# Joining the softmax of two head groups and moving the value products back in a two-layer attention and Fourier kernel

## The chip, the cores and the metric

The kernel runs on one core of a Trainium2 chip. The metric is the device time of one execution in microseconds.

## The reference

The input x has 2048 rows of 640 columns. Four layers follow each other, each adding to x a function of its layer norm: attention, Fourier mixing, attention, Fourier mixing, with the same weights in both of a kind.

```python
x = x + _A_ref(_layernorm(x), A_wqkv, A_wo)
x = x + _B_ref(_layernorm(x), ...)      # and both once more
# _A_ref: 32 heads of 20 columns; row s looks at rows s, s-2, ..., s-14
logits = einsum("bhsd,bhswd->bhsw", q, kg) * scale      # 8 keys per row
attn = softmax(where(mask, logits, -1e9));  o = einsum("bhsw,bhswd->bhsd", attn, vg);  o @ wo
# _B_ref: real part of a DFT over columns and rows, as matrix products
y = einsum("ts,bse->bte", seq_re, a) - einsum("ts,bse->bte", seq_im, b)
```

## The kernel before

Rows are held in 4 chunks (c) of 4 x 128 rows (j). Matrix products are made in three passes of high and low parts, so each operand is split once by ScalarE (high) and VectorE or GpSimd (low). TensorE makes the query/key/value products (`qkv_mm`, L365: 64 groups of 15 matmuls per attention layer), transposes of 128 x 128 (L330) with the subtraction that yields their low part (`pc_sub`, L338), the output projection (`wo_mm`, L518), and the first product of the Fourier layer that follows (`z_mm`, L976), which is begun before the attention layer has ended.

The local attention itself is elementwise work. Keys and values go out to memory and come back as windows, so that each partition holds 4 rows with the 11 rows that their 8 keys span. A head group u (32 per layer: 8 groups of 4 heads for each chunk) is worked in two halves, jp = 0 and 1. For each half:

- `qk_mul` (L434, VectorE): the query times 8 keys, 1280 elements per partition. GpSimd then adds the two halves of each head's 20 columns (L437), except in the half-steps listed in `WHOLE`.
- `qk_red` (L444, VectorE): sums what is left, 640 elements (1280 for a whole one), to 64 logits.
- `soft` for the group: mask (L459, only chunks 0 and 2), maximum over 8 keys (L461), subtraction (L463), the exponential on ScalarE (L452), sum (L465), reciprocal (L467), weights p (L469).
- `av_mul` (L474, VectorE): p times 8 values, 1280 elements. `av_tree` then sums over the keys, on GpSimd in three steps (L493 to L495), and in one step on VectorE (L490) for the very last half.

The order is written out by hand. `at(step, phase, fn, ...)` enters work into a plan; the plan is then issued by half-step, and in each by the list `PHASES`, so that every engine's queue has a fixed order. The query product of group u and half jp stands in half-step s = 2u + jp, its reduction in s + 1, the softmax in 2u + 2 (mask, maximum, subtraction, exponential) and 2u + 3 (sum, reciprocal, weights), the value product in s + 3. `OUTP` has the half-steps in which finished rows of chunks 0 and 1 are transposed (the projection follows two and three later, `wo_add` L162 one after each), `LNS` those of the layer norm of the next layer, `ZTHIRDS` how many thirds of a z product stand in each half-step (from 49 in the first attention layer, from 50 in the second). The query/key/value products are spread by a loop of their own and end in half-steps 47 and 49.

Query (`qp`), weights (`pp`), maximum, sum and mask lie in one PSUM tile `pq`; the logits `lg` in SBUF, in two buffers; products in four SBUF buffers `pr`, windows in five buffers `win`.

Of the kernel before, what the change touches and what calls it, by code (L numbers as in the profile page):

```python
# [22 lines left out]
DH = 20  # L23
W = 8
# [24 lines left out]
ZTHIRDS = (  # L49
    {49: 3, 50: 3, 51: 2, 52: 1, 53: 2, 54: 1, 56: 3, 57: 6, 58: 3, 59: 4, 60: 2, 61: 1, 62: 3, 63: 4, 64: 1},  # L50
    {50: 3, 51: 5, 52: 1, 53: 1, 54: 1, 55: 1, 56: 5, 57: 4, 58: 3, 59: 3, 60: 1, 61: 1, 62: 4, 63: 2, 64: 4},
)
TA = 65
NWARM = 18
# [23 lines left out]
def tile_layers(ctx: ExitStack, tc: tile.TileContext, x, wqkv, wo, cs, wre, wim, out):  # L78
# [166 lines left out]
    def layer_a(li, stats, handoff, prev):  # L245
# [11 lines left out]
        win = {}  # L257
        lgs = {}
        prq = {}
# [41 lines left out]
        def tp(step, kind, c, j, k0, k1, bank, col=0, tag=None):  # L301
            if step not in pieces:
                pieces[step] = []
                at(step, "peT0", pc_pe, step)
                at(step, "hi", pc_hi, step)
                at(step, "peL2" if step == 46 else "peL", pc_sub, step)
                at(step, "actL", pc_lo, step)
            pieces[step].append((kind, c, j, k0, k1, bank, col, tag))
# [132 lines left out]
        def qk_red(u, jp):  # L441
            if jp == 0:
                lgs[u] = T([P, NJ, W, HE], "lg", bufs=2)
            nc.vector.tensor_reduce(  # L444
                lgs[u][:, 2 * jp : 2 * jp + 2].rearrange("p j w h -> p (j w h)"),
                prq.pop((u, jp)),
                axis=AX.X,
                op=ALU.add,
            )

        def soft_exp(u):
            nc.scalar.activation(lgs[u], lgs[u], AF.Exp, scale=scale)  # L452

        def soft(u, part):
            lg = lgs[u]
            v = nc.vector
            if part == 0 and (u // NE) % 2 == 0:
                mw = bass.AP(tensor=mk.tensor, offset=mk.offset, ap=[mk.ap[0], [1, NJ], [1, W], [0, HE]])
                v.tensor_tensor(lg, lg, mw, op=ALU.add)  # L459
            if part == 1:  # L460
                v.tensor_reduce(mx, lg.rearrange("p j w h -> p j h w"), axis=AX.X, op=ALU.max)  # L461
            if part == 2:
                v.tensor_tensor(lg, lg, mx.unsqueeze(2).to_broadcast([P, NJ, W, HE]), op=ALU.subtract)  # L463
            if part == 3:
                v.tensor_reduce(sm, lg.rearrange("p j w h -> p j h w"), axis=AX.X, op=ALU.add)  # L465
            if part == 4:
                v.reciprocal(sm, sm)  # L467
            if part == 5:
                v.tensor_tensor(pp, lg, sm.unsqueeze(2).to_broadcast([P, NJ, W, HE]), op=ALU.mult)  # L469
                lgs[u] = pp  # L470

        def av_mul(u, jp):
            pr = prod()
            nc.vector.tensor_tensor(  # L474
                pr.rearrange("p j w (h d) -> p j w h d", d=DH),
                lgs[u][:, 2 * jp : 2 * jp + 2].unsqueeze(4).to_broadcast([P, 2, W, HE, DH]),
                wview(u, jp, 1, [[DH, HE], [1, DH]]),
                op=ALU.mult,
            )
            avq[(u, jp)] = pr  # L480

        def av_tree(u, i):
            c = u // NE
            e, jp = half(u, i)
            if e == 0:
                oo[(c, jp)] = T([P, 2, D], f"zo{(2 * c + jp) % 4}")
            pr = avq.pop((u, i))
            o = oo[(c, jp)][:, :, e * FE : (e + 1) * FE]
            if (u, i) == (NG - 1, 1):
                nc.vector.tensor_reduce(o, pr.rearrange("p j w f -> p j f w"), axis=AX.X, op=ALU.add)  # L490
# [4 lines left out]
            g.tensor_tensor(o, pr[:, :, 0], pr[:, :, 1], op=ALU.add)  # L495
# [195 lines left out]
        o = NJ * FE + NJ * W * HE  # L691
        mx = pq[:, o : o + NJ * HE].rearrange("p (j h) -> p j h", j=NJ)
        sm = pq[:, o + NJ * HE : o + 2 * NJ * HE].rearrange("p (j h) -> p j h", j=NJ)
        mk = pq[:, o + 2 * NJ * HE : o + 2 * NJ * HE + SLOTS]
        for i in range(3 if first else 0):
# [40 lines left out]
        for u in range(NG):  # L736
            if u in PAIRED:
                for i in range(2):
                    at(2 * u + i - 2, "dmaw", w_load, u, 0, i)
                    at(2 * u + i + 1, "dmaw", w_load, u, 1, i)  # L740
# [47 lines left out]
        for c, w, xtags in (  # L788
            (2, (52, 53, 54, 55), None),
            (3, (60, 61), ("xa", "xa")),  # L790
        ):
            for j in range(NJ):
                if c == 2:
                    late = j > 2 and not first
                    bank = ("xt", "t0", "t1", "t0" if late else "m0")[j]
                    tp(50 if late else 48, "o", c, j, 0, 3, bank, 0, ("ot", "s1", "r1_2", "r1_2")[j])
                    tp(52, "o", c, j, 3, 5, f"aux{j // 2}", 256 * (j % 2))
                else:
                    tp(58 if j < 2 else TA, "o", c, j, 0, 3, f"aux{j % 2}", 0, ("ot", "s1", "zo0", "zo1")[j])
                    tp(60 if j < 2 else 67, "o", c, j, 3, 5, "aux0" if j < 2 else "pq", 256 * (j % 2))  # L800
                if j < len(w):
                    if xtags:
                        at(58, "dmar", r_load, c, j, xtags[j])
                    at(w[j], "pe3w", wo_mm, c, j, ("aux1", "aux0") if c == 3 else ("aux0", "aux1"))
# [7 lines left out]
        for ph in ("peT0", "hi", "peL", "actL"):  # L812
            plan.pop((67, ph))
        at(66, "pe3w", wo_mm, c, 2, ("aux0", "aux1"), 0, 2, 0, 3)
        for i in range(2):
            at(65, "dmas", *((handoff.cw_load, 0) if first else (handoff.c_get,)), 14 + i)
        at(65, "dmar", r_load, c, 2, "xr")
        at(66, "dmar", r_load, c, 3, "xa")
# [11 lines left out]
        for z in range(len(thirds) // 3):  # L830
            t = thirds[3 * z]
            if first and z in PRE:
                at((46, 47, 49)[z] if z < 3 else max(thirds[3 * z - 7] + 1, t - 3), "dmac", handoff.c_get, z)
            elif first:
# [3 lines left out]
            else:  # L838
                at(min(t - 1, 48 + z) if z < 3 else t - 1, "dmac", handoff.c_get, z)
            for p in range(3):  # L840
                at(thirds[3 * z + p], "pe2" if thirds[3 * z + p] == 52 else "pe3", handoff.z_mm, z, p)
        if first:
            at(62, "dmac", handoff.c_load, 13)
            at(63, "hi", handoff.c_hi, 13)
            at(63, "misc", handoff.c_lo, 13)
        else:
            at(63, "dmac", handoff.c_get, 13)

        PHASES = (
            "peT0 dma evac hi pe peL pe2 peL2 fin red0 dma2 qk sA sB av0 sD red1 sE sC exp evacA actL chi evacO actl sF av1 qc actz"  # L850
            " dmaw dmas misc dmac dmar pe3w pe3"
        ).split()
        with tc.manual_schedule(engines=ENGINES):
            if first:
                prologue_first()
            nc.vector.tensor_copy(mk, mask)
# [4 lines left out]
            pc_pe(67)  # L861
            pc_hi(67)
            pc_lo(67, True)
            wo_mm(c, 2, None, 0, 2, 3)
# [517 lines left out]
```

## Time and profile before

| | before |
|---|---|
| median of 3 runs | 1772.23 us (1769.08 to 1773.06) |
| profiled execution | 1771.33 us |
| its span | 1769.3 us |
| granted TensorE clock, mean | 0.995 |
| TensorE busy | 1736.0 us (98%) |
| VectorE busy | 1388.5 us (78%) |
| ScalarE busy | 810.8 us (46%) |
| GpSimd busy | 624.6 us (35%) |

Busy times are unions over the span of one execution. In the rows below PE is TensorE, PEld its weight loads, DVE VectorE, ACT ScalarE, POOL GpSimd and SP SyncE, which issues most DMAs. A group's row has line, engine, operation, tiles (out<-in), shapes and count, then total busy us and mean ns of one, then the engine's idle time just before them and what ended it. A row of the waits has who waited for whom, us in total, times, and the longest. A timeline row has start and duration in us. A row of the windows view has, for a stretch of the span, each engine's busy time and number of instructions, TensorE's granted clock, the DMA share and GB/s.

### The profile page before, as it was taken

The numbers are of one execution on the slowest core, as the hardware profiler recorded it, in microseconds if no ns is written. First come the engines' busy times: TensorE is split into PE (matmuls) and PEld (weight loads), VectorE is DVE, ScalarE is ACT, GpSimd is POOL, SyncE is SP. The second block draws the span as 40 slices with busy tenths as digits, with TensorE's granted clock in tenths as the row PEclk, the third lists the DMA queues.
The fourth block names the chain that finished last, engine by engine and source line by source line (L and its number), as shares of the span: only waits on it lengthen the run. The fifth ranks groups of instructions, "written<-read, shape, count | busy, mean of one in ns | idle before, by whom it ended". The sixth has DMA issues, their size and how long they took to land.

```text
span 1769.3 us, 26448 instructions
## 1 busy us (share of the span) xinstructions
PE 1736.0 (98%) x8798; PEld 1505.9 (85%) x8798; DVE 1388.5 (78%) x2127; ACT 810.8 (46%) x1686; POOL 624.6 (35%) x587
## 2 busy tenths in 40 slices
PE   9999998989999999999999999999999999999999
PEld 6889897878888888888898889988788888888888
DVE  5999999977767767767548999999777676686673
ACT  4654544554445445445534344444434443443441
POOL 3899988850000000000028998899200000000000
PEclk9999999999999999999999999999999999999999
DMA  7996769858777787786657866698688767867761
GB/s 269 309 325 212 220 202 311 274 170 277 274 254 232 243 269 232 246 270 222 206 185 223 264 213 219 202 334 275 203 283 290 247 211 243 260 218 239 255 203 53
DMA packets 270760, 426.19 MB, mean 241 GB/s; under 512 B 22528, under 2 KB 149504, under 8 KB 270368
## 3 DMA queue, kind: packets, MB, share of 16 engines
q1 hardware_dynamic: 267424, 422.54, 72.3%
q10 hardware_dynamic: 3200, 1.97, 0.4%
q8 instruction: 70, 1.15, 0.3%
q14 instruction: 66, 0.54, 0.1%
HBM read 339.28 MB, written 85.14 MB: 240 GB/s over the span
## 4 chain that ended last, share of the span: by engine, by line
PE 59%; DVE 20%; DMA 9%; POOL 5%; issue 4%; ACT 3%; SPq 0%; DVEq 0%; ACTq 0%; POOLq 0%
PE aux L1058 13%; PE t L1147 11%; PE m L1147 11%; PE m L365 9%; PE pq L1147 5%; PE xt L1147 5%; DVE pr L434 4%; DVE pr L474 3%; DMA xc<-stg 3%; PE aux L518 3%; DVE lg L444 2%; POOL pr L493 2%; DMA win<-kvb 1%; POOL pr L437 1%; DVE stg L1111 1%
## 5 line engine op out<-in xcount | busy, mean ns | idle before, releaser
L365 PE MATMUL m<-r,s 128*128 128x480 f32 x1920 | 436.2, 381 | 2.7 <-ACT r L129 2.2
L365 PEld LDWEIGHTS m<-r,s 128*128 128x128 f32 x1920 | 355.4, 188 | 56.3 <-ACT r L129 2.7
L1058 PE MATMUL aux<-r2a,zo 128*128 128x320 f32 x768 | 226.5, 310 | 0.0
L1140 ACT CAST r<-win 128x512 fp32r<-128x512 f32 x246 | 150.5, 620 | 158.4 <-DVE win L1176 75.4
L493 POOL TENSOR_TENSOR pr<-pr 128x640 f32<-128x640 f32 x126 | 208.2, 1652 | 37.3 <-DVE pr L474 36.7
L1058 PE MATMUL aux<-pr,zo 128*128 128x320 f32 x704 | 208.3, 308 | 0.0
L177 POOL TENSOR_TENSOR stats<-stats,mhalf 128x1 f32<-128x1 f32 (+1 forms) x40 | 29.0, 726 | 493.8 <-ACT stats L173 484.7
L1141 DVE TENSOR_TENSOR r<-win,r 128x512 fp32r<-128x512 f32 x246 | 166.3, 688 | 45.0 <-ACT r L1140 43.8
L434 DVE TENSOR_TENSOR pr<-pq,win 128x1280 f32<-128x1280 f32 x128 | 189.7, 1483 | 9.7 <-ACT stg L372 4.8
L474 DVE TENSOR_TENSOR pr<-pq,win 128x1280 f32<-128x1280 f32 x128 | 190.7, 1491 | 4.9
L437 POOL TENSOR_TENSOR pr<-pr 128x640 f32<-128x640 f32 x118 | 168.8, 1431 | 16.2 <-DVE pr L434 15.7
L1147 PE MATMUL m<-r,r 128*128 128x512 f32 x594 | 152.6, 392 | 0.0
L1058 PEld LDWEIGHTS aux<-r2a,zo 128*128 128x128 f32 x768 | 144.1, 188 | 2.0
L1147 PE MATMUL t<-r,r 128*128 128x512 f32 x498 | 135.1, 393 | 1.7 <-PE t L1147 1.7
L1058 PEld LDWEIGHTS aux<-pr,zo 128*128 128x128 f32 x704 | 132.2, 188 | 2.1
L1147 PEld LDWEIGHTS m<-r,r 128*128 128x128 f32 x594 | 111.4, 188 | 24.7
L976 PE MATMUL m<-s,r 128*128 128x512 f32 x384 | 119.8, 400 | 4.0 <-DVE zo L1038 1.5
L976 PE MATMUL t<-s,r 128*128 128x512 f32 x384 | 118.2, 395 | 0.3 <-DVE ot L1033 0.3
L494 POOL TENSOR_TENSOR pr<-pr 128x320 f32<-128x320 f32 x126 | 111.8, 887 | 9.9
L444 DVE TENSOR_REDUCE lg<-pr 128x64 f32<-128x640 f32 (+1 forms) x128 | 110.5, 863 | 4.7 <-POOL pr L437 4.6
L1147 PEld LDWEIGHTS t<-r,r 128*128 128x128 f32 x498 | 93.4, 188 | 23.7 <-PE t L1147 2.5
L372 ACT COPY stg<-m 128x480 f32<-128x480 f32 x128 | 70.9, 554 | 69.5 <-PE m L365 50.2
(290 smaller groups left out, 3233.1 us busy)
## 6 DMA issues: line engine op xcount, KB each, us to landing
win<-cs_in SPq DMA_DIRECT2D x351, 256.0 KB, 4.3
r<-xc SPq DMA_DIRECT2D x240, 256.0 KB, 4.3
win<-kvb SPq DMA_DIRECT2D x96, 440.0 KB, 5.6
xa<-cs_in SPq DMA_DIRECT2D x121, 256.0 KB, 3.9
win<-kvb SPq DMA_DIRECT2D x64, 360.0 KB, 4.5
xc<-stg SPq DMA_DIRECT2D x40, 512.0 KB, 4.2
kvb<-stg SPq DMA_DIRECT2D x60, 320.0 KB, 5.3
s<-c0b SPq DMA_DIRECT2D x26, 512.0 KB, 6.1
```

The source lines that it names most:

```text
L365: nc.tensor.matmul(mt[g][:, : 3 * F], st[:, a, k], wq[q][:, b, k], start=n == 0, stop=n == 14)
L434: nc.vector.tensor_tensor(pr, q, wview(u, jp, 0, [[1, FE]]), op=ALU.mult)
L437: nc.gpsimd.tensor_tensor(pv[:, :, 0:10], pv[:, :, 0:10], pv[:, :, 10:20], op=ALU.add)
L444: nc.vector.tensor_reduce(lgs[u][:, 2 * jp : 2 * jp + 2].rearrange("p j w h -> p (j w h)"), prq.pop((u, jp)), axis=AX.X, op=ALU.add,)
L474: nc.vector.tensor_tensor(pr.rearrange("p j w (h d) -> p j w h d", d=DH), lgs[u][:, 2 * jp : 2 * jp + 2].unsqueeze(4).to_broadcast([P, 2, ...
L493: g.tensor_tensor(pr[:, :, 0:4], pr[:, :, 0:4], pr[:, :, 4:8], op=ALU.add)
L494: g.tensor_tensor(pr[:, :, 0:2], pr[:, :, 0:2], pr[:, :, 2:4], op=ALU.add)
L976: self.last = nc.tensor.matmul(self.z[t][k], self.xn[c][:, a, j, k * P : (k + 1) * P], self.ct[s][:, b], start=s == 0 and i == 0, stop=s = ...
L1058: self.last = nc.tensor.matmul(self.ym[e][:, :320], zt[(k, a, ri)][:, j2 * P : (j2 + 1) * P], w[:, e * 320 : (e + 1) * 320], start=(k, a, ...
L1140: nc.scalar.copy(hi, raw)
L1141: nc.vector.tensor_tensor(lo, raw, hi.bitcast(F32), op=ALU.subtract)
L1147: nc.tensor.matmul(bank, w(a, kb), hl[b], start=start and (a, b) == (0, 0), stop=stop and (a, b) == (1, 0),)
```

## The change

- The logits of two neighbouring groups (u even and u + 1) go into one buffer `lgr`, and mask, maximum, subtraction, exponential, sum and reciprocal are issued once for both, in half-steps 2u + 2 and 2u + 3 of the odd group. The weights p are still made group by group (`soft_p`).
- The value product of half-step s moves from s + 3 to s + 5, the load of its window with it. Output projections of chunks 0 to 3, layer norms, z products and their loads stand two half-steps later; a layer has two half-steps more. The query/key/value products stay.
- `WHOLE` becomes every fourth half-step (7, 11, ..., 63) in both layers: there VectorE reduces all 1280 elements, without GpSimd's half-add. Before there were 8 such half-steps in the first attention layer and 2 in the second.
- The sums over keys go to VectorE for two halves of a layer instead of one.
- In `PHASES` the sum, reciprocal and weights now stand ahead of the reduction of the same half-step.

```diff
-OUTP = (((20, 24, 28, 32), (36, 40, 44, 46)), ((20, 24, 28, 32), (36, 40, 44, 46)))
-LNS = ((40, 52), (42, 52))
+OUTP = (((22, 26, 30, 34), (38, 42, 46, 48)), ((22, 26, 30, 34), (38, 42, 46, 48)))
+LNS = ((42, 54), (44, 54))
-WHOLE = ((43, 45, 47, 49, 51, 55, 57, 59), (51, 57))
+WHOLE = ((7, 11, 15, 19, 23, 27, 31, 35, 39, 43, 47, 51, 55, 59, 63), (7, 11, 15, 19, 23, 27, 31, 35, 39, 43, 47, 51, 55, 59, 63))
 ZTHIRDS = (
-    {49: 3, 50: 3, 51: 2, 52: 1, ...
+    {51: 3, 52: 3, 53: 2, 54: 1, ...
...
         def qk_red(u, jp):
-            if jp == 0:
-                lgs[u] = T([P, NJ, W, HE], "lg", bufs=2)
+            n = 2 * W * HE
             nc.vector.tensor_reduce(
-                lgs[u][:, 2 * jp : 2 * jp + 2].rearrange("p j w h -> p (j w h)"),
+                lgr[:, u % 2, jp * n : (jp + 1) * n],
...
-        def soft_exp(u):
-            nc.scalar.activation(lgs[u], lgs[u], AF.Exp, scale=scale)
+        def soft_exp():
+            nc.scalar.activation(lgr, lgr, AF.Exp, scale=scale)
         def soft(u, part):
+            cols = lgr.rearrange("p b (j w h) -> p (b j) h w", j=NJ, w=W)
...
             if part == 1:
-                v.tensor_reduce(mx, lg.rearrange("p j w h -> p j h w"), axis=AX.X, op=ALU.max)
+                v.tensor_reduce(sm, cols, axis=AX.X, op=ALU.max)
...
             if part == 3:
-                v.tensor_reduce(sm, lg.rearrange("p j w h -> p j h w"), axis=AX.X, op=ALU.add)
+                v.tensor_reduce(sm, cols, axis=AX.X, op=ALU.add)
             if part == 4:
                 v.reciprocal(sm, sm)
-            if part == 5:
-                v.tensor_tensor(pp, lg, sm.unsqueeze(2).to_broadcast([P, NJ, W, HE]), op=ALU.mult)
-                lgs[u] = pp
+        def soft_p(u):
+            lg = lgr[:, u % 2].rearrange("p (j w h) -> p j w h", j=NJ, w=W)
+            r = sm[:, u % 2 * NJ : (u % 2 + 1) * NJ]
+            nc.vector.tensor_tensor(pp, lg, r.unsqueeze(2).to_broadcast([P, NJ, W, HE]), op=ALU.mult)
...
-            if (u, i) == (NG - 1, 1):
+            if i and u >= NG - 2:
                 nc.vector.tensor_reduce(o, pr.rearrange("p j w f -> p j f w"), axis=AX.X, op=ALU.add)
                 return
...
+        lgr = T([P, 2, NJ * W * HE], "lg")
...
                 at(2 * u - 2, "dmaw", w_load, u, 0)
-                at(2 * u + 1, "dmaw", w_load, u, 1)
+                at(2 * u + 3, "dmaw", w_load, u, 1)
...
-                at(s + 3, "av0" if jp else "av1", av_mul, u, jp)
-                at(s + 3, "av0" if jp else "av1", av_tree, u, jp)
-            for i, ph in enumerate(("sA", "sB", "sC")):
-                at(2 * u + 2, ph, soft, u, i)
-                at(2 * u + 3, ("sD", "sE", "sF")[i], soft, u, 3 + i)
-            at(2 * u + 2, "exp", soft_exp, u)
+                at(s + 5, "av0" if jp else "av1", av_mul, u, jp)
+                at(s + 5, "av0" if jp else "av1", av_tree, u, jp)
+            at(2 * u + 5, "sF", soft_p, u)
+            if u % 2:
+                for i, ph in enumerate(("sA", "sB", "sC")):
+                    at(2 * u + 2, ph, soft, u, i)
+                for i, ph in enumerate(("sD", "sE")):
+                    at(2 * u + 3, ph, soft, u, 3 + i)
+                at(2 * u + 2, "exp", soft_exp)
...
-        last = 66
+        last = 68
...
-            "peT0 dma evac hi pe peL pe2 peL2 fin red0 dma2 qk sA sB av0 sD red1 sE sC exp evacA actL chi evacO actl sF av1 qc actz"
+            "peT0 dma evac hi pe peL pe2 peL2 fin red0 dma2 qk sA sB av0 sD sE sF red1 sC exp evacA actL chi evacO actl av1 qc actz"
             " dmaw dmas misc dmac dmar pe3w pe3"
```

More of the change, by code (lines that the diff above doesn't have):

```diff
@@ L257, in layer_a @@
         win = {}
-        lgs = {}
         prq = {}
@@ L305, in tp @@
                 at(step, "hi", pc_hi, step)
-                at(step, "peL2" if step == 46 else "peL", pc_sub, step)
+                at(step, "peL2" if step == 48 else "peL", pc_sub, step)
                 at(step, "actL", pc_lo, step)
@@ L795, in layer_a @@
                     bank = ("xt", "t0", "t1", "t0" if late else "m0")[j]
-                    tp(50 if late else 48, "o", c, j, 0, 3, bank, 0, ("ot", "s1", "r1_2", "r1_2")[j])
-                    tp(52, "o", c, j, 3, 5, f"aux{j // 2}", 256 * (j % 2))
-                else:
-                    tp(58 if j < 2 else TA, "o", c, j, 0, 3, f"aux{j % 2}", 0, ("ot", "s1", "zo0", "zo1")[j])
-                    tp(60 if j < 2 else 67, "o", c, j, 3, 5, "aux0" if j < 2 else "pq", 256 * (j % 2))
+                    tp(52 if late else 50, "o", c, j, 0, 3, bank, 0, ("ot", "s1", "r1_2", "r1_2")[j])
+                    tp(54, "o", c, j, 3, 5, f"aux{j // 2}", 256 * (j % 2))
+                else:
+                    tp(60 if j < 2 else TA, "o", c, j, 0, 3, f"aux{j % 2}", 0, ("ot", "s1", "zo0", "zo1")[j])
+                    tp(62 if j < 2 else 69, "o", c, j, 3, 5, "aux0" if j < 2 else "pq", 256 * (j % 2))
                 if j < len(w):
                     if xtags:
-                        at(58, "dmar", r_load, c, j, xtags[j])
+                        at(60, "dmar", r_load, c, j, xtags[j])
                     at(w[j], "pe3w", wo_mm, c, j, ("aux1", "aux0") if c == 3 else ("aux0", "aux1"))
@@ L812, in layer_a @@
         for ph in ("peT0", "hi", "peL", "actL"):
-            plan.pop((67, ph))
-        at(66, "pe3w", wo_mm, c, 2, ("aux0", "aux1"), 0, 2, 0, 3)
+            plan.pop((69, ph))
+        at(68, "pe3w", wo_mm, c, 2, ("aux0", "aux1"), 0, 2, 0, 3)
         for i in range(2):
-            at(65, "dmas", *((handoff.cw_load, 0) if first else (handoff.c_get,)), 14 + i)
-        at(65, "dmar", r_load, c, 2, "xr")
-        at(66, "dmar", r_load, c, 3, "xa")
+            at(67, "dmas", *((handoff.cw_load, 0) if first else (handoff.c_get,)), 14 + i)
+        at(67, "dmar", r_load, c, 2, "xr")
+        at(68, "dmar", r_load, c, 3, "xa")
         if prev is not None:
@@ L855, in layer_a @@
                 prologue_first()
-            nc.vector.tensor_copy(mk, mask)
+            nc.vector.tensor_copy(
+                mk.rearrange("p (j w) -> p j w", j=NJ),
+                bass.AP(tensor=mask.tensor, offset=mask.offset, ap=[mask.ap[0], [1, NJ], [1, W]]),
+            )
             for s in range(LEAD0[0], last + 1):
@@ L860, in layer_a @@
                         fn(*args)
-            pc_pe(67)
-            pc_hi(67)
-            pc_lo(67, True)
+            pc_pe(69)
+            pc_hi(69)
+            pc_lo(69, True)
             wo_mm(c, 2, None, 0, 2, 3)
```

43 lines of the change are left out of this document (22 added, 21 removed).

## The prediction

> **What bounds the kernel now.** I read the page first, then the windows view cut at the borders of the stages, then VectorE's timeline over one step pair, the groups by form, and the waits by stage.
>
> ```profile
> span 1769.3 us, 26448 instructions
> PE 1736.0 (98%) x8798; PEld 1505.9 (85%) x8798; DVE 1388.5 (78%) x2127; ACT 810.8 (46%) x1686; POOL 624.6 (35%) x587
> ```
> ```profile
> core 0: us, PE busy (x) PEld busy (x) DVE busy (x) ACT busy (x) POOL busy (x), PEclk, DMA share, GB/s
> 35.30:279.40 244.10, 239.13 (x1233) 210.83 (x1232) 232.96 (x321) 131.81 (x328) 217.87 (x201) 1.00 0.80 257
> 279.40:359.10 79.70, 73.98 (x387) 64.70 (x388) 75.50 (x111) 35.78 (x91) 68.32 (x65) 0.96 0.82 279
> 918.90:960.10 41.20, 41.20 (x200) 35.76 (x199) 34.21 (x47) 14.94 (x33) 28.83 (x26) 1.00 0.71 226
> 960.10:1160.70 200.60, 200.03 (x1057) 178.49 (x1055) 191.47 (x272) 86.17 (x213) 182.99 (x168) 1.00 0.73 231
> 1160.70:1232.30 71.60, 68.24 (x361) 59.59 (x362) 66.97 (x101) 32.71 (x84) 66.05 (x62) 0.98 0.90 309
> ```
>
> Over the span TensorE looks like the only bound. The windows say more. I cut them where a query product starts. The first attention layer runs from half-step 0 (35.30) to 49 (279.40), where the first Fourier product (z) is planned, and on to 63 (359.10); the second from half-step 0 (918.90) over 9 (960.10) and 50 (1160.70, its first z) to 63 (1232.30). In the stretches ahead of z three engines are full together: in 960.10:1160.70 TensorE 99.7%, VectorE 95%, GpSimd 91%. Only from 918.90 to 960.10 is TensorE alone: VectorE works 34.21 of 41.20 us there. So a change of VectorE's load ahead of z counts, unless TensorE is behind it.
>
> VectorE's order, over half-steps 20 and 21 of the second layer:
>
> ```profile
> 1011.30 1.48 DVE L434 TENSOR_TENSOR pr<-pq,win 128x1280 f32<-128x1280 f32 x1
> 1012.82 0.39 DVE L461 TENSOR_REDUCE pq<-lg 128x16 f32<-128x128 f32 x1
> 1013.24 1.49 DVE L474 TENSOR_TENSOR pr<-pq,win 128x1280 f32<-128x1280 f32 x1
> 1014.65 0.28 DVE L463 TENSOR_TENSOR lg<-lg,pq 128x128 f32<-128x128 f32 x1
> 1014.85 1.48 DVE L434 TENSOR_TENSOR pr<-pq,win 128x1280 f32<-128x1280 f32 x1
> 1016.43 0.39 DVE L465 TENSOR_REDUCE pq<-lg 128x16 f32<-128x128 f32 x1
> 1016.73 0.81 DVE L444 TENSOR_REDUCE lg<-pr 128x64 f32<-128x640 f32 x1
> 1017.46 0.26 DVE L467 RECIPROCAL pq<-pq 128x16 f32<-128x16 f32 x1
> 1017.75 0.29 DVE L469 TENSOR_TENSOR pq<-lg,pq 128x128 f32<-128x128 f32 x1
> 1018.08 1.49 DVE L474 TENSOR_TENSOR pr<-pq,win 128x1280 f32<-128x1280 f32 x1
> 1019.51 0.82 DVE L444 TENSOR_REDUCE lg<-pr 128x64 f32<-128x640 f32 x1
> 1020.25 1.48 DVE L434 TENSOR_TENSOR pr<-pq,win 128x1280 f32<-128x1280 f32 x1
> ```
>
> Instructions overlap, so I cost them by the distance from start to start. The pair takes 1020.25 - 1011.30 = 8.95 us with no wait in it, four half-steps 17.90. Softmax's own distances: maximum 0.42, subtraction 0.20, sum 0.30, reciprocal 0.29, weights (L469) 0.33.
>
> **Softmax of two groups.** Wider forms are not in the trace; their slopes come from these groups:
>
> ```profile
> L444 DVE TENSOR_REDUCE lg<-pr 128x64 f32<-128x640 f32 x118 | 95.7, 811 | 4.7 <-POOL pr L437 4.6
> L465 DVE TENSOR_REDUCE pq<-lg 128x16 f32<-128x128 f32 x64 | 25.2, 394 | 8.1 <-ACT lg L452 2.0 <-ACT xa L194 0.5
> L461 DVE TENSOR_REDUCE pq<-lg 128x16 f32<-128x128 f32 x64 | 25.0, 391 | 2.1
> L444 DVE TENSOR_REDUCE lg<-pr 128x64 f32<-128x1280 f32 x10 | 14.8, 1476 | 0.0
> L490 DVE TENSOR_REDUCE zo<-pr 128x160 f32<-128x1280 f32 x2 | 4.7, 2360 | 0.1
> ```
>
> Where the reduced elements are neighbours (the two L444), an element costs (1476 - 811) / 640 = 1.04 ns. Where they lie apart, as in the maximum (stride 4) and in L490 (stride 80), it is (2360 - 391) / 1152 = 1.71 ns. The new maximum and sum reduce 256 elements at stride 4, so I take 128 x 1.71 = 0.22 us more each; the lower end, at the neighbours' slope, is 0.13. The subtraction grows by 128 x 1.04 = 0.13, the reciprocal, of 16 elements more, by an estimated 0.10 (between 0 and its own 0.26); the mask, in half of the groups, I set even. The exponential widens on ScalarE:
>
> ```profile
> L452 ACT ACTIVATE lg<-lg 128x128 f32<-128x128 f32 x64 | 20.1, 314 | 141.7 <-DVE lg L463 141.7
> ```
>
> It runs under the query product of 1.48 us that follows the subtraction. Only behind the last pair no query product follows; there it shows, at 0.31 us or up to twice that.
>
> [...]
>
> The order matters too. Reciprocal now follows the sum at once and needs its result, so the sum shows in full: 0.39 + 0.22 + 0.04 = 0.65 instead of twice 0.30. The next reduction writes where the weights' instruction has just read; the built program makes it wait, so that instruction still costs 0.33. Four half-steps then are: 1.52 + 0.64 + 1.41 + 0.33 = 3.90; 1.58 + 0.65 + 0.39 + 0.33 + 0.73 + 1.43 + 0.74 = 5.85; 1.41 + 1.41 = 2.82; 1.52 + 0.33 + 0.73 + 1.43 + 0.74 = 4.75. Sum 17.32: 0.58 saved.
>
> **Every fourth query product whole.** The reduction grows from 811 to 1476 ns: 0.67 per four half-steps. So VectorE's pace is 17.99 against 17.90, 0.09 slower: one edit pays for the other. GpSimd loses its half-add (L437), a quarter of them. What VectorE waited for it goes to nothing: 2.1 us in the first layer, 0.8 in the second.
>
> ```profile
> DVE lg L444 <- POOL pr L437: 2.1, 4, 0.9
> ```
> ```profile
> DVE pr L434 <- ACT pq L407: 1.6, 2, 1.5
> DVE r L910 <- ACT r L906: 1.0, 2, 0.5
> DVE lg L444 <- POOL pr L437: 0.8, 2, 0.6
> ```
>
> The first fence holds all of VectorE's waits between 60 and 299 us, the second the longest between 960 and 1160 us.
>
> **Two half-steps later.** The query/key/value products keep their steps and end at 47 (first layer) and 49. Out-projections, norms and z move by two together, with their loads, and keep their order on the SP queue. Only a group's value window is now issued behind the key window and the query of the group after next. It costs nothing while two half-steps (8.95 us) cover its landing, 5.6 us in the middle; without that cover VectorE's value product and all behind it would wait, as once for a key window:
>
> ```profile
> win<-kvb SPq DMA_DIRECT2D x96, 440.0 KB, 5.6
> ```
> ```profile
> DVE pr L434 <- DMA win<-kvb: 0.7, 1, 0.7
> ```
>
> But between the last key/value product and z TensorE now has two half-steps with little more than 15 matmuls of 2.36 us each, against 3.55 and 5.40 us of VectorE. And z can't come early, because the out-projection ahead of it waits for VectorE's addition:
>
> ```profile
> 270.20 2.36 PE L518 MATMUL aux<-r2a,ot 128*128 128x320 f32 x15
> ...
> 279.52 2.47 PE L518 MATMUL aux<-r2a,s 128*128 128x320 f32 x15 [0.45 <-DVE xr L162]
> 281.83 1.56 PE L976 MATMUL m<-s,r 128*128 128x512 f32 x6
> ```
>
> So z starts when VectorE has gone through two more half-steps: +8.95. From this, per layer:
> - First layer: the value products that half-steps 3 and 4 no longer hold free 2 x 1.41 = 2.8 (0 if TensorE were behind there; VectorE's 232.96 of 244.10 says it is mostly not). The old order had three whole sums by then (43, 45, 47), now inside the pace: -2.0. Pace 11.5 x 0.09 = +1.0; GpSimd's waits -2.1. Sum 8.95 - 2.8 - 2.0 + 1.0 - 2.1 = **+3.0**.
> - Second layer: its start is TensorE's (34.21 of 41.20), so the freed 2.8 only become idle time and count nothing. No whole sum stood ahead of z. Pace 10 x 0.09 = +0.9; GpSimd's waits -0.8; of the 2.6 on ScalarE I take half, -1.3. Sum 8.95 + 0.9 - 0.8 - 1.3 = **+7.7**.
>
> **From z on** the same matmuls follow, and TensorE sets the pace (73.98 of 79.70 and 68.24 of 71.60 busy), so VectorE's lighter load brings little: between 0 and the 9 us of gaps, I take -1.5, since most gaps wait for transposes that move along. **The tail** loses stalls on GpSimd:
>
> ```profile
> PE aux L330 <- POOL zo L495: 3.5, 2, 2.8
> PE pq L330 <- POOL zo L495: 1.7, 1, 1.7
> PE m L976 <- POOL s L963: 1.3, 1, 1.3
> ```
>
> Of these 2.8, 1.7 and 1.3 stand in the two tails, 5.8 together. GpSimd has no half-add left there, but VectorE now sums two value products whole (2360 ns each) and comes late in its place: between 0 and -5.8, I take -3.4.
>
> **Sum:** 3.0 + 7.7 - 1.5 - 3.4 = +5.8 us. The profiled execution took 1771.33 us (span 1769.3 and 2.0 around it), 0.9 below the median of 1772.23. So 1771.3 + 5.8 = 1777.1. A measurement of this kernel can tell about 0.2% from no change, 3.5 us.
>
> **Rivals.**
> - The strided reductions widen at the neighbours' slope: 2 x 0.09 less per pair, over 21.5 pairs 3.9 us, total +1.9, 1773. The 391 ns for 128 elements, far over what 1.04 ns each explain beside L444's remainder of 146 ns, speak against. [...] With half of the tail's gain lost it ends at 1775, still within 0.2%. Chance of such an end 0.22.
> - Faster: TensorE is the bound throughout (98%) and brings a backlog to the last key/value product, so that the two half-steps hide behind it. It decides from a backlog of 9 us on. Then z does not move, and 1.5 + 5.8 us of gaps go: 1764. For it: 200.03 of 200.60 us busy ahead of the second layer's z. Against: the 0.45 us above, where TensorE, out of other work, waits for VectorE two products ahead of z. Chance 0.18.
> - Slower still: the waits on GpSimd and ScalarE are not theirs but TensorE's delay passed on, so that with a lighter VectorE they come back elsewhere, and the tail's do too. It decides if TensorE lies behind VectorE through the middle of the layers: 8.95 + 8.95 + 1.9 - 2.0 = +17.8, 1789. Chance 0.10.
> - That the change is not made: the built program has 142 fewer VectorE instructions, the wide forms and the moved products; none.
>
> **How the numbers follow.** The forecast, 1775 to 1784, has 0.50. Slower by over 0.2% is 0.50 + 0.10 = 0.60, within 0.2% 0.22, faster 0.18. The range for 8 in 10 leaves out the far halves of the two outer cases: 1766 to 1787.
>
> **What would show it.** Right: maximum and sum at about 0.61 us, a step of four at 17.9 to 18.1 us between query products; GpSimd gone from VectorE's waits; TensorE's gaps grown by some 3 and 8 us just ahead of the first z product of each layer, and shrunk in the tails. Wrong: z starting no later after half-step 0 than now; the wide reductions near 0.52; new waits of VectorE for the exponential.

## The result, and the profile after

The changed kernel takes 1782.22 us (median of 4 runs, 1779.23 to 1784.03), the kernel before 1770.65 us (4 runs, 1767.85 to 1773.06): the ratio is 1.0063 with a 95% interval from 1.0048 to 1.0077, so it is slower, by about 11 us. The profiled run of the changed kernel is the fastest of its four (1779.23 us), and its span is only 7.6 us longer than before:

```profile
span 1776.9 us, 26242 instructions
PE 1740.0 (98%) x8798; PEld 1507.9 (85%) x8798; DVE 1385.7 (78%) x1985; ACT 804.8 (45%) x1654; POOL 589.6 (33%) x561
```

The small operations first, from VectorE's groups by form. Against the rows of the prediction, maximum (L461) and sum (L466) cost 622 and 624 ns for twice the elements, the reciprocal (L468) 366, and thirty query products are summed whole (L442 over 1280 elements):

```profile
L442 DVE TENSOR_REDUCE lg<-pr 128x64 f32<-128x640 f32 x98 | 80.1, 817 | 10.8 <-POOL pr L436 4.9
L442 DVE TENSOR_REDUCE lg<-pr 128x64 f32<-128x1280 f32 x30 | 44.3, 1476 | 0.0
L466 DVE TENSOR_REDUCE pq<-lg 128x32 f32<-128x256 f32 x32 | 20.0, 624 | 6.1 <-ACT lg L450 2.7 <-ACT ot L352 0.5
L461 DVE TENSOR_REDUCE pq<-lg 128x32 f32<-128x256 f32 x32 | 19.9, 622 | 1.0
L468 DVE RECIPROCAL pq<-pq 128x32 f32<-128x32 f32 x32 | 11.7, 366 | 1.1
```

In the timeline the query products of half-steps 20 and 24 of the second layer stand 18.11 us apart (no mask there); with a mask in between it is 18.4 (18.3 before).

```profile
1014.85 1.48 DVE L433 TENSOR_TENSOR pr<-pq,win 128x1280 f32<-128x1280 f32 x1
...
1032.96 1.48 DVE L433 TENSOR_TENSOR pr<-pq,win 128x1280 f32<-128x1280 f32 x1
```

VectorE's waits in the middle of the layers, 60 to 285 us and 963 to 1169 us: GpSimd is gone from them.

```profile
DVE pr L433 <- ACT pq L406: 1.0, 2, 0.6
```
```profile
DVE pr L433 <- ACT pq L406: 0.3, 1, 0.3
```

Now the place of the loss. The windows view cut at the first z product, first the kernel before (two rows of the first layer, one of the second), then the changed one:

```profile
core 0: us, PE busy (x) PEld busy (x) DVE busy (x) ACT busy (x) POOL busy (x), PEclk, DMA share, GB/s
34.50:281.80 247.30, 242.21 (x1252) 213.82 (x1251) 235.27 (x323) 133.88 (x332) 220.99 (x204) 1.00 0.80 257
281.80:365.00 83.20, 76.27 (x394) 65.85 (x392) 78.93 (x113) 38.26 (x97) 71.74 (x69) 0.96 0.81 276
...
961.30:1162.70 201.40, 199.13 (x1052) 177.78 (x1051) 192.20 (x274) 87.48 (x216) 183.63 (x170) 1.00 0.73 232
```
```profile
34.50:290.20 255.70, 247.22 (x1253) 218.00 (x1252) 241.97 (x277) 133.77 (x324) 214.21 (x199) 0.98 0.79 255
290.20:365.00 74.80, 70.82 (x381) 61.80 (x380) 67.82 (x91) 34.89 (x86) 69.17 (x65) 1.00 0.78 270
...
963.80:1170.20 206.40, 200.67 (x1053) 177.81 (x1051) 200.18 (x234) 86.68 (x208) 177.97 (x167) 1.00 0.73 233
```

The first layer's first z product comes 8.4 us later. TensorE's idle time ahead of it grew from 5.1 to 8.5 us; the other 5.0 us are busy time for one matmul more, and the granted clock says why: 0.98 in place of 1.00. In slices of 3.40 us:

```profile
275.20:278.60 3.40, 3.40 (x18) 3.32 (x17) 3.23 (x6) 1.06 (x3) 3.39 (x3) 0.56 0.87 233
278.60:282.00 3.40, 0.28 (x3) 0.04 (x1) 3.30 (x6) 2.43 (x5) 3.26 (x4) 0.94 1.07 402
282.00:285.40 3.40, 3.29 (x11) 3.02 (x12) 3.40 (x4) 2.73 (x8) 3.24 (x4) 0.50 1.02 393
285.40:288.80 3.40, 3.40 (x16) 3.40 (x15) 3.19 (x6) 0.00 (x0) 3.40 (x3) 0.56 0.84 291
```

A slice in which TensorE did nearly nothing is followed by two at about half the clock, and a shorter dip stands ahead of it. The kernel before has such a dip too, but behind its first z product (0.96 in its second row, 1.00 in the changed kernel's). These 5.0 us are not all delay of z: part of them is time in which TensorE would else have waited (see the first layer below). In the second layer z starts 5.0 us later counted from the layer's first query/key/value product, 3.5 us of it idle time of TensorE (2.27 to 5.73 in the rows).

Ends of the layers, from the timelines (the second layer counted from its first query/key/value product):

| kernel | ratio to before | layer 1: first z begins, last z ends | layer 2: first z begins, last z ends |
|---|---|---|---|
| before | 1 | 281.8, 395.6 | 293.8, 397.7 |
| changed | 1.0063 | 290.2, 396.4 | 298.8, 402.8 |
| e11, half-steps alone | 1.0046 | 294.7, 400.9 | 300.5, 403.7 |
| e1, with value products | 1.0094 | 293.7, 403.0 | 299.6, 402.8 |
| e2, with pairing | 1.0107 | 295.6, 404.6 | 302.6, 405.8 |
| e3, whole sums alone | 1.0081 | 287.2, 401.6 | 297.7, 406.3 |
| e12, copy moved in layer 2 | 1.0069 | 291.8, 402.7 | 298.8, 403.2 |
| e6, layout | 1.0035 | 290.5, 398.6 | 297.7, 402.5 |
| e13, layout, weights, copy | 1.0014 | 287.2, 395.3 | 295.3, 399.0 |
| e10, before with layout | 0.9970 | 281.7, 394.7 | 292.4, 395.1 |

In the profiled run the first layer's loss is nearly given back by the last z product (+0.8). That is this run: e12 has the same instructions in the first layer, and there the last z product comes 7.1 us later than before. So one profile tells a stage to several us, no better.

### The profile page after: what moved, and what is told of

Its sections match the earlier page's. It is cut to its first block, busy times and chain, and to the rows that moved or that the text cites. A ratio compares the mean times of both kernels' runs of the same rounds, so it can differ in the third digit from the quotient of the medians.

```text
span 1776.9 us, 26242 instructions
## 1 busy us (share of the span) xinstructions
PE 1740.0 (98%) x8798; PEld 1507.9 (85%) x8798; DVE 1385.7 (78%) x1985; ACT 804.8 (45%) x1654; POOL 589.6 (33%) x561
## 3 DMA queue, kind: packets, MB, share of 16 engines
q10 hardware_dynamic: 3200, 1.97, 0.4%
q8 instruction: 70, 1.15, 0.3%
## 4 chain that ended last, share of the span: by engine, by line
PE 55%; DVE 12%; DMA 5%; issue 3%; POOL 2%; ACT 1%; SPq 0%; DVEq 0%; ACTq 0%; POOLq 0%
PE aux L1067 14%; PE t L1156 11%; PE m L1156 10%; PE pq L1156 5%; PE xt L1156 5%; PE m L364 3%; DVE pr L477 3%; DMA xc<-stg 3%; DVE pr L433 2%; PE aux L521 2%; PE m L985 1%; PE t L985 1%; DVE lg L442 1%; POOL pr L496 1%; DMA win<-cs_in 1%
## 5 line engine op out<-in xcount | busy, mean ns | idle before, releaser
L496 POOL TENSOR_TENSOR pr<-pr 128x640 f32<-128x640 f32 x124 | 200.5, 1617 | 63.9 <-DVE pr L477 63.9
L477 DVE TENSOR_TENSOR pr<-pq,win 128x1280 f32<-128x1280 f32 x128 | 189.7, 1483 | 3.3
L436 POOL TENSOR_TENSOR pr<-pr 128x640 f32<-128x640 f32 x98 | 142.0, 1449 | 26.3 <-DVE pr L433 26.1
L442 DVE TENSOR_REDUCE lg<-pr 128x64 f32<-128x640 f32 (+1 forms) x128 | 124.4, 972 | 10.8 <-POOL pr L436 4.9
L371 ACT COPY stg<-m 128x480 f32<-128x480 f32 x128 | 70.9, 554 | 93.7 <-PE m L364 70.4
```

The lines of the kernel that those rows point to most:

```text
L436: nc.gpsimd.tensor_tensor(pv[:, :, 0:10], pv[:, :, 0:10], pv[:, :, 10:20], op=ALU.add)
L442: nc.vector.tensor_reduce(lgr[:, u % 2, jp * n : (jp + 1) * n], prq.pop((u, jp)), axis=AX.X, op=ALU.add,)
L477: nc.vector.tensor_tensor(pr.rearrange("p j w (h d) -> p j w h d", d=DH), pp[:, 2 * jp : 2 * jp + 2].unsqueeze(4).to_broadcast([P, 2, W, H ...
```

## Experiments

Theory D: the loss is the delay itself, two more VectorE half-steps ahead of z, with little for TensorE to do in them. Rival P: the price of the wide reductions and the whole sums.

### e11: the half-steps alone

The kernel before, with only the plan of what follows the value products taken from the changed one:

```diff
-OUTP = (((20, 24, 28, 32), (36, 40, 44, 46)), ...
+OUTP = (((22, 26, 30, 34), (38, 42, 46, 48)), ...
-LNS = ((40, 52), (42, 52))
+LNS = ((42, 54), (44, 54))
...
```

> The kernel before with nothing changed but the half-steps of what follows the value products: transposes, output products, norms, z and the tails two half-steps later; softmax, value products and whole sums as before. Theory D (z waits for two more VectorE half-steps, whatever the value products do): the first z product 6 to 12 us later in layer 1 and 5 to 9 us in layer 2, and 8 to 17 us slower as a whole, like the kernel with the two half-steps alone (1790). Rival V (the value products' own delay costs it: their windows land too late, or the start of a layer): within 4 us of the kernel before.

Measured: 1783.71 us against 1775.04, ratio 1.0046 (1.0029 to 1.0063). Softmax, value products and whole sums are the old ones, and the first z product comes 12.9 and 6.7 us later. So two half-steps more by themselves cost most of what the change costs, without pairing and without whole sums: theory D is shown to that extent. Two things stay open. In e11 the end of the layer moves together with the start of z, and no run here separates the two. And of the 12.9 us, 2.8 stand already at half-step 20 (106.8 us after half-step 0, 104.0 before), where nothing of the plan differs yet.

### e1, e2, e3: the parts one on the other

```diff
 # e1: changed kernel, softmax group by group, old WHOLE
-                v.tensor_reduce(sm, cols, axis=AX.X, op=ALU.max)   # 256 elements
+                v.tensor_reduce(r, cols, axis=AX.X, op=ALU.max)    # 128 elements
 # e2: changed kernel; e3: kernel before
-WHOLE = ((7, 11, 15, ..., 63), (7, 11, 15, ..., 63))   # e2
+WHOLE = ((43, 45, 47, 49, 51, 55, 57, 59), (51, 57))   # e2; e3 the other way round
```

> The changed kernel with only the two half-steps kept: softmax goes group by group again (each reduction over 128 elements a partition), and the whole sums stand at the kernel before's places. Theory D (delay): what the change costs is the two VectorE half-steps between the last q/k/v product and the first z product of each layer, which TensorE can't fill. Then this kernel is nearly as slow as the changed one: 7 to 13 us over the kernel before (1777 to 1784), the first z product 6 to 9 us later in layer 1 and 5 to 8 us in layer 2, four half-steps in the middle of a layer unchanged near 17.9 us. Rival P (price): the delay is hidden, and the wider reductions and the whole sums cost it; then this kernel is within 3 us of the kernel before. Rival T (TensorE has a backlog up to the first z product): as P, and TensorE shows no stalls of over 1 us ahead of the first z product.

> The changed kernel with the whole query sums at the kernel before's ten places in place of thirty. Theory D: the delay stays, so it is still slower than the kernel before by 4 to 10 us; four half-steps in the middle fall from 18.1 to about 17.5 us (0.66 less), but TensorE sets the pace there for most of the time, so that no more than 4 us of it shows; VectorE's waits for GpSimd come back (0.2 to 1 us a piece). Rival P with the whole sums as the price: eleven of them lie in layer 2's stretch from 964 us to the first z product, 11 x 0.66 = 7 us less than the changed kernel, level with the kernel before.

> The kernel before with only the thirty whole query sums. Theory D: no delay, so near the kernel before: VectorE works 0.66 us more in four half-steps (18.5 for 17.9), of which the stretch where VectorE sets the pace shows some: 0 to 5 us slower; no wait for GpSimd in the middle of a layer. Rival P (whole sums are the price): 7 us slower or more, in the stretch of layer 2 from 960 us to the first z product above all.

Measured: e1 1789.79, e2 1791.66, e3 1788.46 us against 1772.88; ratios 1.0094 (1.0077 to 1.0112), 1.0107 (1.0094 to 1.0120), 1.0081 (1.0066 to 1.0097). All three are slower than the changed kernel's 1.0063; e1 and e3 go beyond what theory D expected. In e1 the two layers hold 12.5 us of the 18.0 by which its span is longer than before; the other 5.5 lie in the Fourier stages, whose code is the same, and stay unexplained. Beside e11, e1 has the value products moved as well. The layers of the two differ by 2.1 and -0.9 us (see the table), and the rest of the 5.3 us between their spans lies in the Fourier stages, so a cost of the moved value products (rival V) is not seen.

e3 was given 0 to 5 us by theory D and 7 or more by rival P, and took 15.6 us more. On the kernel before, the thirty whole sums are a price indeed.

e2 missed too, and tells most. With the old whole sums a step of four was expected at 17.5 us. It takes 19.3, and VectorE waits for GpSimd once in each (waits from 962 to 1165 us, then two rows of the timeline):

```profile
DVE lg L442 <- POOL pr L436: 11.3, 11, 1.5
```
```profile
1006.21 0.82 DVE L442 TENSOR_REDUCE lg<-pr 128x64 f32<-128x640 f32 x1 [1.50 <-POOL pr L436]
...
1025.55 0.82 DVE L442 TENSOR_REDUCE lg<-pr 128x64 f32<-128x640 f32 x1 [1.53 <-POOL pr L436]
```

Softmax of pairs leaves half-steps of 2.8 and of 5.9 us on VectorE, while GpSimd needs 4.4 in each (a half-add of 1.42, three sums of 1.57, 0.88 and 0.53). So pairing alone hands the pace to GpSimd. The whole sums take a half-add from it in every fourth half-step and hand the pace back to VectorE. In e3, without pairing, the same sums only load VectorE: no wait for GpSimd is left, but a step of four in the stretch from half-step 8 to 20 of the second layer takes 18.9 us (18.3 before). So the sums cost where VectorE sets the pace, and gain where pairing has made GpSimd set it (1.0063 with them, 1.0107 without). Pairing by itself makes no clear difference (1.0107 beside 1.0094 of e1). Together the two are even with e11 (1.0063 beside 1.0046, intervals overlapping) and a little better than e1.

### e4: query/key/value products later too

```diff
-TWICE = ((8, 10, 12, 14, 16, 18), (10, 14, 18, 20))
+TWICE = ((8, 10, 12, 14), (10, 14))
```

> The changed kernel with two half-steps fewer that carry two q/k/v products: these products end two half-steps later (at 49 and 51 rather than 47 and 49), as the first z product does, so that TensorE's work ahead of z is spread over the same half-steps as VectorE's. Theory D: TensorE's stalls ahead of the first z product shrink, and 2 to 6 us of the loss come back: 1774 to 1779. Rival P: TensorE's place in the stretch doesn't matter, and the time is the changed kernel's within 2 us. If the later q/k/v products make window loads late, it is slower than the changed kernel, with VectorE's waits for win in the second half of a layer.

Measured: 1786.42 us, ratio 1.0082 (1.0065 to 1.0099). A miss: TensorE's idle time in the 40 us ahead of z goes from 5.0 and 4.2 us to 0.9 and 0.6, but z starts no earlier (291.2 and 298.8), and the last z comes 4.3 and 4.5 us later than in the changed kernel. So TensorE's idle time there was not itself the loss; its work, put later, delays what follows. As the last sentence of the expectation has it, VectorE also waits for a window, 4.5 us behind the second layer's first z:

```profile
DVE pr L433 <- DMA win<-kvb: 4.5, 1, 4.5
```

### e5, e8, e9: z back at the old half-steps

```diff
+SOON = (7, 15)                    # e8, e9: (7, 15, 23, 27, 31)
-                at(s + 5, "av0" if jp else "av1", av_mul, u, jp)
+                d = 3 if u in SOON else 5
+                at(s + d, "av0" if jp else "av1", av_mul, u, jp)
```

> The changed kernel with its z products, transposes and output products ahead of z back at the kernel before's half-steps (first z product at 49 and 50 rather than 51 and 52). To make that possible the second group of the pairs (6, 7) and (14, 15) has its weights and value products two half-steps earlier than the others, beside those of the first group, with its weights written in place in the pair's tile. Work on VectorE and GpSimd is the same. Theory D (the loss is the two VectorE half-steps ahead of z): the first z product comes 6 to 9 us earlier than in the changed kernel (layer 1 near 281 us, layer 2 near 290 us after its first q/k/v product rather than 298.8), and 4 to 8 us of the whole come back: 1774 to 1778. Rival R (z's start doesn't matter, the end of a layer is set by VectorE's last half-steps): z earlier, but the last z product where it was, 1780 to 1784.

> The changed kernel's paired softmax and thirty whole query sums, with everything behind the value products (transposes, output products, z, tails) at the kernel before's half-steps: the second groups of the pairs (6, 7), (14, 15), (22, 23), (26, 27), (30, 31) have their weights and value products two half-steps earlier than the others. Theory D: the delay is gone from the ends of the layers too, the pace is that of the changed kernel (18.1 to 18.4 us against 18.3), so the time is the kernel before's or a little better: 1764 to 1774. Rival P (pairing and whole sums cost something themselves): 1777 to 1783. Where two value products stand in one half-step, GpSimd's six sums in a row may hold VectorE by 1 to 3 us each.

> The kernel with everything behind the value products at the kernel before's half-steps, and the logits laid out head by head besides. Theories D and S together: 1 to 5 us less than that kernel without the layout, 1761 to 1772, faster than both the kernel before and the changed one.

In e8 and e9 the transposes of half-step 65 read group 30's first value sums before they are written; instructions and their number are as described. Measured: e5 1797.28, e8 1824.79, e9 1821.76 us against 1775.83, ratios 1.0119 (1.0102 to 1.0136), 1.0288 (1.0266 to 1.0310), 1.0264 (1.0248 to 1.0280). They miss, and don't test theory D: two value products in one half-step have a price of their own. A step of four that holds them takes 21.9 us in place of 18.4, the next 1.0 less. And the value product that reads its weights in place is slower, though shape and strides are the same (from e5):

```profile
L479 DVE TENSOR_TENSOR pr<-lg,win 128x1280 f32<-128x1280 f32 x8 | 15.0, 1872 | 0.0
```

The others read them from `pq` at 1483 ns. The weights lie in SBUF in the first case and in PSUM in the second.

### e6, e10: the stride

```diff
-            cols = lgr.rearrange("p b (j w h) -> p (b j) h w", j=NJ, w=W)
+            cols = lgr.rearrange("p b (x w) -> p (b x) w", w=W)      # laid out (h j w)
```

> The changed kernel with the logits laid out head by head (h, j, w), so that maximum and sum read neighbours in place of elements 16 bytes apart. Theory S (what the wide reductions cost over their neighbours' slope is the stride): both fall from 622 ns to 450 to 520 ns, the query reduction that now writes 128 bytes apart stays within 5%, and four half-steps become 0.2 to 0.35 us shorter; 1 to 5 us of the whole. Rival (the price is of the instruction's form, not of the stride): 622 ns as before, and the same time.

> The kernel before with its logits laid out head by head (h, j, w), softmax still group by group; the weights' instruction reads neighbours and writes 16 bytes apart. Theory S (the stride costs the reductions): maximum and sum fall from 392 ns to about 250 to 300 ns, 0.2 to 0.3 us less per group, 0.4 to 0.6 us per four half-steps against 18.3 us. Where VectorE sets the pace with nothing beside it, that is 3 to 6 us of the whole. Rival G (GpSimd sets the same pace: its four sums take 4.41 us of each half-step of 4.57): VectorE gets waits for GpSimd instead, and no more than 2 us come of it. Rival: the weights' strided writes cost what the reductions gain, same time.

Measured: e6 1781.43 us against 1775.83, ratio 1.0035 (1.0021 to 1.0049); e10 1770.35 against 1775.04, ratio 0.9970 (0.9955 to 0.9985). VectorE's groups by form, e6 first, then e10:

```profile
L471 DVE TENSOR_TENSOR pq<-lg,pq 128x128 f32<-128x128 f32 x64 | 25.6, 400 | 2.1
L464 DVE TENSOR_REDUCE pq<-lg 128x32 f32<-128x256 f32 x32 | 13.7, 427 | 5.8 <-ACT lg L449 2.4 <-ACT ot L352 0.5
L460 DVE TENSOR_REDUCE pq<-lg 128x32 f32<-128x256 f32 x32 | 13.7, 427 | 1.0
```
```profile
L470 DVE TENSOR_TENSOR pq<-lg,pq 128x128 f32<-128x128 f32 x64 | 18.9, 296 | 2.2
L461 DVE TENSOR_REDUCE pq<-lg 128x16 f32<-128x128 f32 x64 | 18.9, 295 | 2.1
L466 DVE TENSOR_REDUCE pq<-lg 128x16 f32<-128x128 f32 x64 | 18.8, 294 | 8.0 <-ACT lg L452 2.0 <-ACT xa L194 0.5
```

The reductions fall from 622 to 427 and from 392 to 295 ns: the stride of four elements costs 0.76 ns an element over neighbours. In e6 the weights' instruction reads the logits 128 bytes apart (and its reciprocals 16 bytes apart) and takes 400 ns for 296, half of the gain; in e10 it writes 16 bytes apart, into PSUM, and pays nothing. e10 is faster than both kernels, by 0.3% than the kernel before.

### e12, e13: the wait ahead of the second layer's z

In the changed kernel TensorE's transposes end at 1166.2, and the next step waits for a cast on ScalarE. ScalarE stands at the query copy (L406), which waits for VectorE's value product, and statistics queued behind it come before the cast:

```profile
1165.71 0.49 PE L329 MATMUL t<-ident,zo 128*128 128x128 f32 x3
1169.71 0.69 PE L337 MATMUL t<-r,nident 128*128 128x384 f32 x1 [3.51 <-ACT r L333]
```
```profile
1167.44 0.43 ACT L406 COPY pq<-qs 128x320 f32<-128x320 f32 x1 [2.65 <-DVE pr L477]
...
1169.19 0.46 ACT L333 CAST r<-t 128x384 fp32r<-128x384 f32 x1
```
```diff
-            at(2 * u - 1, "qc", q_copy, u)
+            at(*((2 * u, "red0") if ly and u == 26 else (2 * u - 1, "qc")), q_copy, u)
```

> The changed kernel with one copy moved: in the second layer ScalarE's copy of the query of group 26, which waits for VectorE's last product of half-step 51, stands behind the casts of the transposes of half-step 52 and no longer ahead of them. Theory Q (the wait that ends last ahead of z is this copy: VectorE's half-step reaches z through ScalarE's order): TensorE's stall of 3.67 us ahead of the second layer's first z product shrinks to about 1 us, z starts some 2 to 3 us earlier after the layer's first query product (246 us rather than 248.8), and the whole gains 1 to 3 us at most (1779 to 1781). Rival (the casts wait for the transposes' own data): no change in the stall.

> The changed kernel with that copy moved, the logits laid out head by head, and the weights' instruction reading neighbours and writing 16 bytes apart. Maximum and sum near 428 ns, the weights back at 296 ns (399 where it read 128 bytes apart): four half-steps 0.4 us shorter than in the changed kernel, 18.0 us where it took 18.4. Theory D (two VectorE half-steps ahead of z are what remains): 4 to 9 us less than the changed kernel, still 2 to 8 us over the kernel before. Rival P (the price lay in the wide reductions): level with the kernel before or faster.

Measured: e12 1785.67 us against 1775.19, ratio 1.0069 (1.0053 to 1.0086): no gain. e12's rows:

```profile
1172.75 0.49 PE L329 MATMUL t<-ident,zo 128*128 128x128 f32 x3
1173.97 0.44 PE L337 MATMUL t<-r,nident 128*128 128x384 f32 x1 [0.73 <-ACT r L333]
1176.85 2.93 PE L985 MATMUL m<-s,r 128*128 128x512 f32 x6 [2.44 <-DMA s<-c0b]
```

The wait for the cast did shrink from 3.51 to 0.73 us, as expected of theory Q, and now a wait of 2.44 us for a load of z's table (s<-c0b) stands ahead of z. z starts 248.8 us after the first query product, as it did.

e13 takes 1777.39 us, ratio 1.0014 (1.0003 to 1.0025): level with the kernel before within the 0.2% that counts, 0.5% under the changed kernel. Maximum and sum are at 428 ns, the weights at 296, a step of four at 18.1 with a mask and 17.7 without (18.4 and 18.1 in the changed kernel). e13 differs from e12 in the layout and the weights' instruction alone, on the same chip, and takes 8.3 us less. So 0.4 us of VectorE's time in four half-steps is worth some 8 us of the whole: VectorE sets the pace. Between theory D (2 to 8 us over the kernel before) and rival P (level) the 2.2 us measured do not decide.

## Why the prediction was right, and where it was not

- **Direction and range** held: 1782.2 lies between 1766 and 1787, and slower had 0.60. The size was under-estimated, +5.8 us for a measured 11 us or so (7.6 between the profiled runs). That it came as near is in part luck. In the profiled runs the parts ahead of z, +3.0 and +7.7 in the forecast, are +8.4 and +5.0, and the stretches from first to last z are 7.5 us shorter together where -4.9 was forecast: three misses that make up for each other.
- **Strided slope**: right. 0.61 us was predicted for maximum and sum, 0.62 measured; the rival at the neighbours' slope (0.52) falls. e6 shows that it is the stride: the same reductions over neighbours take 427 ns. So the pattern decides between 622 and 427 ns for the same 256 elements; by what mechanism no run here shows.
- **Pace**: 17.99 predicted, 18.11 measured (without a mask). Reciprocal (+0.11) and whole sum (1476 ns) were as predicted. The weights' instruction was priced at 0.33; from start to start it is 0.39 to 0.40, twice in four half-steps, which is the difference.
- **GpSimd's waits** went from the middle of the layers, as predicted. That without the whole sums pairing would have raised them to 11.3 us in the second layer (e2) was not foreseen.
- **z waits for VectorE**: right, and shown by e11 without the rest; the TensorE-backlog rival falls, since z moved later in every kernel with these half-steps. The slower rival's 1789 did not come; freed time that turns into waits, its mechanism, shows at the first layer's start alone.
- **First layer**: +3.0 predicted, +8.4 measured at the first z product (9.2 counted from half-step 0, which comes 0.8 us earlier). The step that failed first is the 2.8 us from value products that half-steps 3 and 4 no longer hold. Half-step 20 stands at 138.31, 103.83 us after half-step 0 (34.48), and before at 139.27, 103.99 after 35.28: nothing is left of the 2.8. The time turns into a wait. Half-step 4 begins 19.9 us after half-step 0, before 20.2, and there VectorE now waits 2.73 us for ScalarE, which copies TensorE's q/k/v products (L371) and has waited for TensorE itself (half-step 4 of the kernel before, then two rows of the changed one):

```profile
55.47 1.48 DVE L434 TENSOR_TENSOR pr<-pq,win 128x1280 f32<-128x1280 f32 x1
```
```profile
49.44 0.56 ACT L371 COPY stg<-m 128x480 f32<-128x480 f32 x1 [2.19 <-PE m L364]
...
54.42 1.49 DVE L433 TENSOR_TENSOR pr<-pq,win 128x1280 f32<-128x1280 f32 x1 [2.73 <-ACT stg L371]
```

  TensorE works without a pause between the two in both kernels (busy for all of the 4.98 us from 49.44 to 54.42, and before for all of the 6.07 from 49.40 to 55.47), which is the case that the prediction put in brackets. The first 48 half-steps are 2.8 us shorter (237.1 for 239.9) where 5.9 were forecast.

  The second failure is that the two half-steps were priced at the mean, 8.95. Counted from half-step 48 to the one in which z stands, they add 9.6 us in the first layer and 10.5 in the second. Half-steps 48 and 49 are long in every kernel: 10.7 and 9.9 us before, 10.6 and 11.4 in the changed kernel, 10.3 and 13.2 in e11 with its softmax group by group; so it is not the pairing that makes them so.

  The third is that no term held the clock, and it is smaller than the 5.0 us of longer matmuls. z begins 4.8 us after the start of its half-step, before and in e11 2.4 us, and the thirty matmuls of the out-projection ahead of z take 6.67 us where two times fifteen took 2.36 each: some 2.4 us. In e12, with the same instructions in this layer, TensorE is busy for 1.8 us less ahead of z, and z still begins 256.2 us after half-step 0 (255.8 in the changed kernel).
- **Second layer**: +7.7 predicted, +5.0 measured. Out-projection additions and norms that moved to later half-steps left VectorE's first 48 half-steps 4.5 us shorter (227.3 for 231.8); e11, which has that move and the old softmax, has 225.9. The prediction gave 1.2 for that stretch.
- **Tails**: TensorE's waits for GpSimd fell from 5.8 to 0.9 us, and the whole value sums on VectorE show 0.3: 4.6 us of waits less, for a predicted gain of 3.4. As time this is not seen in the second layer, nor is the 1.5 from z on: from first to last z it takes 103.9 us before and 104.0 after. In the first layer that stretch is 7.6 us shorter in the profiled run and 2.9 in e12.

```profile
PE aux L329 <- POOL zo L498: 0.9, 1, 0.9
...
PE pq L329 <- DVE zo L493: 0.3, 1, 0.3
```

Left open: the spread of the first layer between runs of the same instructions (+0.8 and +7.1), and the 5.5 us in e1's Fourier stages. The spread is not the clock's: to the last z TensorE is busy for 347.2 us in the changed kernel and for 347.5 in e12, and what differs is its idle time.

## What to carry to other kernels

Three engines are full together here, and an edit that relieved one handed the pace to the next: whole sums cost 0.8% on the kernel before and gained 0.4% on the paired one, so test such edits in combination. The later start of the next stage was paid in the half-steps that stand just there (9.6 and 10.5 us), not in the mean (8.95). And a wait taken away may only uncover the transfer behind it (in e12 3.51 us became 0.73, and a load was then waited for 2.44 us): look for what is late next before counting the gain.

## What was not expected of the hardware

- TensorE's granted clock fell to 0.50 behind a pause of 3.23 us (ended at 282.11), and already behind one of 1.72 us (ended at 272.95), but not behind one of 2.87 us:

```profile
303.48 0.38 PE L337 MATMUL aux<-ot,nident 128*128 128x256 f32 x1 [2.87 <-ACT s L333]
```

  In the traces of the kernel before and of the changed one the clock changes only at the borders of stretches of 3.41 us: in the changed kernel it falls at 274.76, 281.58, 373.74 and 1169.05 us, for one or two stretches, before at 295.66, 370.75 and 1162.65. Counted on these stretches, the ends of the kernels left aside, each of the five at full clock in which TensorE was busy for 0.55 to 1.15 us was followed by one at 0.50. Of those with 1.8 to 2.1 us two were (from 271.34, busy for 1.80, and from 370.33, 2.07) and five were not (1.80, 1.95 and 1.97 in the changed kernel, 2.07 and 2.10 before), and none with more was. So the length of a pause alone does not tell: the one of 2.87 us was shared by two stretches (rows 3 and 4; the first two show a fall).

```profile
278.20:281.60 3.40, 0.68 (x6) 0.44 (x4) 3.26 (x7) 2.03 (x4) 3.24 (x5) 1.00 1.07 396
281.60:285.00 3.40, 2.89 (x9) 2.62 (x10) 3.40 (x3) 3.13 (x9) 3.24 (x4) 0.50 1.04 404
298.70:302.10 3.40, 1.92 (x13) 1.45 (x11) 3.30 (x4) 1.01 (x4) 2.02 (x2) 1.00 0.95 330
302.10:305.50 3.40, 1.97 (x9) 1.58 (x10) 2.44 (x2) 3.08 (x12) 3.17 (x6) 1.00 1.01 333
```

  A stretch ahead of a fall is not wholly idle: TensorE is busy for 0.68 us in the first row.

- VectorE's weights' instruction took 400 ns for 128 elements with logits read from SBUF 128 bytes apart, and the same 296 as with neighbours when it wrote into PSUM 16 bytes apart. The query reduction, writing its 64 results into SBUF 128 bytes apart, took 819 ns for 817.
- The same product took 1872 ns with its weights in SBUF, where the windows lie too, and 1483 with them in PSUM; why was not tried.
